# Attention kernel with a recorded schedule: the third bank of a ScalarE group lent to VectorE, another unit order, and scheduler constants by stage

## Chip, cores, metric

One core of one Trainium2 chip. The metric is the device time of one execution in microseconds.

## The reference, cut to what matters

Four attention layers run in turn over 2048 tokens of width 512, with 32 heads of 16: A, B, A, B with the same weights twice. A attends within segments of 512 tokens under a causal mask and adds a linear memory of earlier segments. B attends over all 2048 tokens.

```python
x = x + _A_ref(_layernorm(x), A_wq, A_wk, A_wv, A_wo, A_beta)
x = x + _B_ref(_layernorm(x), B_wqkv, B_wo)
x = x + _A_ref(_layernorm(x), A_wq, A_wk, A_wv, A_wo, A_beta)
x = x + _B_ref(_layernorm(x), B_wqkv, B_wo)
# in B: scores = q @ k^T * Dh**-0.5 ; p = softmax(scores) ; o = p @ v     (A: the same in segments, masked, plus memory)
```

The exponentials of the scores are most of the work: 32 heads of 2048 x 2048 for each B layer.

## The kernel before

The program is recorded by a scheduler in Python. It keeps a clock for each engine, advances them by constants, and at each step picks what TensorE issues next: a group of score tiles, a PV batch (the matmuls of four finished tiles with V), or a step of a background thread (projections, layer norm, memory). The order that it records is then fixed: each engine executes its own list in order, held by semaphores. A wrong constant makes no wrong result, only an order that suits the chip badly.

PSUM has eight banks: two halves of three for score groups, two for projections and for accumulating PV. TensorE fills one half while ScalarE reads the other.

```python
DX_AHEAD = 0.696; DX_SLACK = 4.004; MMC = 0.22; PV0 = 0.33; PB = 0.027; DVE_AHEAD = 4.525; RATE = 0.762; CF = 0.684   # (cut; one line each)
PAT = ["AAAAAAAA", "ABABABABBBABAAABBA", "AAAABBBBAAAA", "AAABABABABAA", "AAABABABABAA", "BBABAABAAA"]   # order of units in each block

def form(self):                                   # the next group for ScalarE (cut)
    n = 3 if m == "w" or self.half == 0 else 2    # "w": threes; else threes and twos in turn

def emit_group(self, tiles, mode):                # (cut)
    # a score matmul for each tile, each into a bank of its own and on its own 32 rows of the array
    self.dx_scores(tiles, mode)                   # perhaps one more tile, for VectorE
    # ONE activation over all the banks of the group
    o = sc.add("act", lambda e: e.activation(dst, src, ACT.Exp, scale=float(SCALE)), ...)

def dx_scores(self, tiles, mode):                 # (cut)
    bank = self.free_bank()
    t = sc.t["pe"]
    if bank.t_free + 0.3 > t or sc.t["dve"] > t + self.dx_ahead(...) or not self.dx_room():
        return
    self.dx_score([x["pv"][0][2] for x in tiles], bank, SC1)    # one matmul, one VectorE eviction
```

After four such evictions VectorE computes the batch's exponential in seven operations over 2048 columns (`g_dx`), and the batch's PV joins the queue.

The softmax here doesn't subtract the row's maximum and nothing guards it: scores larger than these inputs give would overflow.

Of the kernel before, what the change touches and what calls it, by code (L numbers as in the profile page):

```python
# [25 lines left out]
EXP_C = SCALE * 1.4426950408889634  # L26
EXP_A, EXP_B, EXP_D = 10.0720224, 43.9353157, 125.459638
DX_AHEAD = 0.696
DX_SLACK = 4.004
DX_LEAD = 69  # L30
MMC = 0.22
SC0, SC1 = 0.33, 0.02
PV0 = 0.33
PB = 0.027
DVE_AHEAD = 4.525
MAXPV = 3
RATE = 0.762
LAST = 3
HAM_W = 3.4133
HAM_T = 5.0  # L40
# [4 lines left out]
CF = 0.684  # L45
# [1 line left out]
T_ISS = 1.3  # L47
D_LAT = 2.5
QMASK = True
PAT = ["AAAAAAAA", "ABABABABBBABAAABBA", "AAAABBBBAAAA", "AAABABABABAA", "AAABABABABAA", "BBABAABAAA"]  # L50
M3 = "m"
LN_G = 3
DX_WIDE = True


class Op:
# [227 lines left out]
class KernelBuilder:  # L284
# [810 lines left out]
            tl["nblk"] = {"0": 4, "13": 4, "22": 4}[tl["masks"]]  # L1095
        return u

    def emit_group(self, tiles, mode):
        sc = self.sc
        self.mode = mode  # L1100
        lo = self.bank_lo
        banks = [self.banks[lo + i] for i in range(len(tiles))]
        alloc = self.new_alloc()
        n = len(tiles)
        s0 = self.slot_for(n)
        self.slot = s0 + n
        for k in range(max(len(tl["sc"]) for tl in tiles)):
            for i, tl in enumerate(tiles):
                if k >= len(tl["sc"]):
                    continue  # L1110
                lhsT, rhs, off, N, reads = tl["sc"][k]
                out = self.ps[:, banks[i].col0 + off:banks[i].col0 + off + N]
                sc.add("pe", (lambda out, lhsT, rhs: lambda e: e.matmul(out, lhsT, rhs, start=True, stop=True))(out, lhsT, rhs),  # L1113
                       reads=reads, bank_ops=[(banks[i], "w", alloc)], emit=False, name="S", cost=((SC0 if k == 0 else N / 2400.0) if i == 0 else SC1),
                       cold=N / 2400.0 if i == 0 else 0.0, work=0.14 * N / 512)
        self.dx_scores(tiles, mode)
        W = 512 * n
        src = self.ps[:, banks[0].col0:banks[0].col0 + W]
        dst = self.pT[:, s0:s0 + n, :].rearrange("p a b -> p (a b)")
        o = sc.add("act", lambda e: e.activation(dst, src, ACT.Exp, scale=float(SCALE)), writes=[self.b_pT[s0 + i] for i in range(n)],  # L1120
                   bank_ops=[(b, "r", alloc) for b in banks], name="E", cost=0.065 + W / 1200.0)
        for b in banks:
            b.t_free = o.t_end
        t_rdy = o.t_end
        i = 0
        while i < n:
            m = tiles[i]["masks"]
            k = i + 1
            while m == "0" and k < n and tiles[k]["masks"] == m:
                k += 1  # L1130
            if m is not None:
                if m == "0":
                    ap = self.pT[:, s0 + i:s0 + k, 0:128]
                    pat = [[0, k - i], [1, 128]] if k - i > 1 else [[1, 128]]
                    if k - i == 1:
                        ap = self.pT[:, s0 + i, 0:128]
                    cnt = k - i
                else:
                    base = self.pT[:, s0 + i:s0 + i + 1, 0:1]
                    ap = bcast_ap(base, [[384 if m == "13" else 256, 2], [1, 128]])  # L1140
                    pat = [[0, 2], [1, 128]]
                    cnt = 2
                om = sc.add("pool", (lambda ap, pat: lambda e: e.affine_select(ap, ap, pattern=pat, compare_op=ALU.is_ge, fill=0.0, base=0,  # L1143
                                                                            channel_multiplier=-1))(ap, pat),
                            reads=[self.b_pT[s0 + x] for x in range(i, k)], writes=[self.b_pT[s0 + x] for x in range(i, k)],
                            name="K", cost=0.2 + 0.115 * cnt)
                t_rdy = om.t_end
            i = k
        for i, tl in enumerate(tiles):
            tl["slot"] = s0 + i  # L1150
        for tl in tiles:
            self.slot_use[tl["slot"]] = tl.get("nblk", 1)
            self.pvt.append(tl)
            uu = tl["u"]
            if len(self.pvt) == 4:
                uu["pq"].append(dict(tiles=self.pvt, t=t_rdy, dx=False))
                self.pvt = []
            self.tile_scored(uu)
# [38 lines left out]
    def dx_ahead(self, u, need):  # L1197
# [4 lines left out]
        for tl, _ in self.upq:  # L1202
            if tl["u"]["kind"] == "B" and tl["u"]["no"] > u["no"]:
                break
            n += 1
        return DVE_AHEAD if 0.45 * n < need + DX_SLACK else DX_AHEAD

    def dx_scores(self, tiles, mode):

        sc = self.sc  # L1210
        if ("op", 0, 3) not in self.ev or len(tiles) < 2:
            return
        if self.dx_tiles is None:
            four = self.dx_pick()
            if four is None:
                return
            self.dx_tiles = four
            self.dx_left = [2, 3, 0, 1]
        bank = self.free_bank()
        t = sc.t["pe"]  # L1220
        if bank.t_free + 0.3 > t or sc.t["dve"] > t + self.dx_ahead(self.dx_tiles[0]["u"], 7.5 + 1.4 * len(self.dx_left)) or not self.dx_room():
            return
        self.dx_score([x["pv"][0][2] for x in tiles], bank, SC1)

# [108 lines left out]
    def pv_group(self):  # L1333
# [14 lines left out]
        if u["qm"]:  # L1348
            sc.t["pe"] += 0.1
            for tl in g["tiles"]:  # L1350
                for b in tl["pv"]:
# [3 lines left out]
                    if not g["dx"]:  # L1355
# [3 lines left out]
                                                                                stop=True, skip_group_check=True))(o0, w, v, first),  # L1359
                           reads=[br] + vreads, bank_ops=[(bank, "w", alloc)], emit=False, name="W", cost=PB)  # L1360
                    first = False
            if g["dx"]:
                op.emit = True
        else:
            n = len(g["tiles"][0]["pv"])
            for k, i in ((k, i) for k in range(n) for i in range(4)):
# [5 lines left out]
                else:  # L1372
# [4 lines left out]
                       reads=[br] + vreads, bank_ops=[(bank, "w", alloc)], emit=g["dx"] and i == 3, name="V",  # L1377
                       cost=0.0 if i else PV0 if k == 0 else N / 2400.0, cold=0.0 if i else N / 2400.0, work=0.16 * N / 512)
        if g["dx"]:
# [197 lines left out]
    def units(self):  # L1577
# [3 lines left out]

        seq = [(A(0, 0, "m") + A(0, 1, "m"), [], PAT[0])]
        seq += [(A(0, 2, "m") + A(0, 3, "m"), F(1, 0, 4, "a", "m") + F(1, 4, 8, "m", "m"), PAT[1])]
        seq += [(F(1, 8, 12, "m", "m") + F(1, 12, 16, "b", "w") + B(1, 0, "w", NPART), [], "")]
        for qc in range(1, 4):
            b = B(1, qc, "w")
            seq += [(b, A(2, qc - 1, "w"), PAT[1 + qc])]
        a3 = F(3, 0, 12, "a", M3)
# [5 lines left out]
    def build(self):  # L1594
        self.alloc()
        self.cnt = {}
        self.late = []
        self.slot = 0
        self.slot_use = [0] * RING
        self.pvt = []  # L1600
        self.ln_owner = None
        self.setup()
        self.out_batches = [self.new_batch(f"out{s}") for s in range(4)]
        for L in range(LAST + 1):
            self.spawn_layer(L)
        sc = self.sc
        self.log = []
        self.blocks = [[list(a), list(b), list(pat)] for a, b, pat in self.units()]
        self.blocks = [[[x for x in q if x[0]["L"] <= LAST] for q in b[:2]] + [b[2]] for b in self.blocks]
        for i, (u, _) in enumerate(x for b in self.blocks for x in b[0] + b[1] if x[0]["kind"] == "B"):  # L1610
            u["no"] = i
        self.upq = []
        self.half = 0
        self.mode = "n"
        self.act_ok = True
        self.run()
        self.act_ok = True
        self.acc_bank = None
        self.mode = "n"
        while self.threads:  # L1620
            self.ensure_any()
        for s in range(4):
            bt = self.out_batches[s]
            sc.add("sp", (lambda bt: lambda e: e.wait_ge(bt.sem, bt.total))(bt), name="fin")
        sc.finalize()
# [103 lines left out]
    def run(self):  # L1729
        sc = self.sc  # L1730
        credit = 0.0
        g = None
        while True:
# [4 lines left out]
            t = sc.t["pe"]  # L1738
# [38 lines left out]
            if rs is not None and rs <= t + eps and not (credit >= 1.0 and bg is not None):  # L1777
                tiles, m = g
                self.bank_lo = 3 * self.half
                self.half ^= 1  # L1780
                del self.upq[:len(tiles)]
                L = tiles[0]["u"]["L"]
                self.act_ok = m == "m" and L < 2
                self.emit_group(tiles, m)
                credit = min(credit + (RATE if self.act_ok else 0.0), 2.0)
                self.log.append((len(self.log), L, tiles[0]["u"]["s"], m, round(sc.t["act"], 2), round(sc.t["pe"], 2), round(sc.t["dve"], 2),
                                 round(sc.t["pool"], 2), self.backlog(), len(tiles)))
                g = None
                continue
            if rp is not None and rp <= t + eps and self.backlog() >= MAXPV:  # L1790
# [27 lines left out]
            if KEEP and self.acc_open and t + d <= tc + KEEP_D and (0.0 if sc.warm else KEEP0) <= sc.lately() < KEEP and self.pvu and self.pvu[0]["L"] <= KEEP_L:  # L1818
                self.keep_warm()
                continue  # L1820
            sc.t["pe"] = to

    def keep_warm(self):

# [75 lines left out]
```

## Time and profile before

| | before |
|---|---|
| median of the runs beside the changed kernel | 2096.53 us (2092.73 to 2097.51, 4 runs) |
| span of the profiled run | 2094.3 us |
| busy: ScalarE, TensorE, VectorE | 95%, 83%, 77% |
| score tiles on ScalarE, on VectorE | 4316, 420 |
| ScalarE groups of three, of two | 1312, 188 |

Read it as one bound engine with a feeder: ScalarE's time is its number of tiles and groups times their fixed costs, plus whatever it waits for scores. The lines are in the prediction.

### The profile page before, as it was taken

How to read it: one execution, taken by the hardware profiler on the slowest of the kernel's cores; microseconds unless marked ns; L12 is line 12 of the kernel's file. 1: busy time of each engine (PE TensorE's matmuls, PEld its weight loads, DVE VectorE, ACT ScalarE, POOL GpSimd, SP SyncE). 2: the span in 40 equal slices, each digit the busy share in tenths (PEclk: the TensorE clock that was granted, in tenths of full speed). 3: DMA queues.
4: the chain of work that ended last, by engine and by line, in shares of the span. 5: the costliest groups of instructions: out<-in, count | busy, mean ns of one | idle time of the engine just before them, and what ended most of it. 6: DMA issues, size and time to landing. Idle time of an engine off the chain costs nothing.

```text
span 2094.3 us, 41469 instructions
## 1 busy us (share of the span) xinstructions
PE 1732.3 (83%) x17382; PEld 589.3 (28%) x17382; DVE 1605.0 (77%) x2447; ACT 1997.3 (95%) x1595; POOL 248.1 (12%) x563
## 2 busy tenths in 40 slices
PE   7779988888877888878888888888888888888887
PEld 2222221111221122121222223223444433443443
DVE  6887668886647777777768578688788988897984
ACT  5879989999999999999999999999999999999998
POOL 4542320000130002110021103200000000000000
PEclk9779876567565575576765788575655565555555
DMA  4210100001000000010000100100000000000000
GB/s 121 51 32 11 31 11 1 1 1 21 1 11 11 11 11 1 1 16 18 8 1 1 21 11 1 22 1 2 14 5 4 4 14 4 5 4 14 7 5 11
DMA packets 75467, 27.31 MB, mean 13 GB/s; under 512 B 68112, under 2 KB 74768, under 8 KB 75280
## 3 DMA queue, kind: packets, MB, share of 16 engines
q1 hardware_dynamic: 74176, 23.62, 5.2%
q8 instruction: 136, 2.23, 0.4%
q10 hardware_dynamic: 1104, 1.05, 0.2%
q14 instruction: 51, 0.42, 0.1%
HBM read 6.30 MB, written 2.10 MB: 4 GB/s over the span
## 4 chain that ended last, share of the span: by engine, by line
ACT 48%; PE 30%; issue 10%; DVE 9%; POOL 1%; DMA 1%; SPq 0%; ACTq 0%; DVEq 0%; POOLq 0%
ACT pT L1120 47%; PE ps L1113 12%; PE ps L610 8%; PE ps L1358 5%; PE ps L1376 4%; PE ps L1246 2%; POOL pT L1143 1%; DMA xT<-xn 1%; DVE T L1496 1%; DVE lnst L647 1%; DVE dz L1249 1%; DVE ot L904 0%; DVE ph L771 0%; SPq L429 0%; DVE df L1286 0%
## 5 line engine op out<-in xcount | busy, mean ns | idle before, releaser
L1120 ACT ACTIVATE pT<-ps 128x1536 bf16<-128x1536 f32 (+1 forms) x1504 | 1962.6, 1487 | 69.0 <-PE ps L1113 59.3
L1113 PE MATMUL ps<-q,kB 32*128 32x512 bf16 x3676 | 696.0, 548 | 262.3 <-ACT pT L1120 254.5
L1249 DVE TENSOR_SCALAR dz<-ps 128x512 int32<-128x512 f32 x420 | 289.8, 690 | 153.5 <-PE ps L1246 139.5
L1113 PEld LDWEIGHTS ps<-q,kB 32*128 32x128 bf16 x3676 | 129.9, 97 | 698.5 <-ACT pT L1120 648.7
L1376 PE MATMUL ps<-pT,vB 128*17 128x512 bf16 x2228 | 286.0, 515 | 2.3 <-DVE ot L904 1.3
L1143 POOL TENSOR_SCALAR_AFFINE_SELECT pT<-pT 128x256 bf16<-128x256 bf16 (+2 forms) x515 | 219.5, 455 | 549.2 <-ACT pT L1120 547.9
L1246 PE MATMUL ps<-q,kB 32*128 32x512 bf16 x420 | 243.3, 579 | 0.0
L1358 PEld LDWEIGHTS ps<-vB,pT 128*128 128x128 bf16 x5792 | 181.2, 104 | 169.9 <-issue 169.3
L1358 PE MATMUL ps<-vB,pT 128*128 128x17 bf16 x5792 | 214.2, 176 | 0.0
L1113 PE MATMUL ps<-q,kA 32*128 32x512 bf16 (+3 forms) x1024 | 125.0, 391 | 40.4 <-ACT pT L1120 38.6
L1286 DVE TENSOR_SCALAR df<-dz 128x2048 f16<-128x2048 uint16 x105 | 129.3, 1232 | 3.0
L1376 PEld LDWEIGHTS ps<-pT,vB 128*17 128x17 bf16 x2228 | 52.1, 90 | 204.7 <-issue 191.4
L1293 DVE TENSOR_SCALAR db<-dz 128x2048 int16<-128x2048 int16 x77 | 94.0, 1221 | 2.8 <-PE ps L1376 2.8
L1496 DVE STREAM_TRANSPOSE T<-ps 128x512 f32<-128x512 f32 x94 | 66.6, 709 | 24.7 <-PE ps L1376 24.2
L610 PE MATMUL ps<-xT,wB 128*128 128x512 bf16 x256 | 80.1, 445 | 0.8 <-DVE dz L1249 0.8
L610 PE MATMUL ps<-xT,wA 128*128 128x512 bf16 x256 | 73.6, 417 | 6.0 <-DVE T L1496 2.0
L976 DVE TENSOR_TENSOR x_tok<-x_tok,ps 128x512 bf16<-128x512 bf16 x60 | 41.1, 686 | 42.4 <-PE ps L610 42.3
L655 POOL TENSOR_SCALAR lnr<-lnmv 128x4 f32<-128x4 f32 x15 | 5.2, 344 | 550.1 <-DVE lnmv L650 550.1
L1298 DVE TENSOR_TENSOR tokk<-tokk,df 128x2048 f16<-128x2048 f16 x57 | 69.5, 1219 | 0.7
L1302 DVE TENSOR_TENSOR tokk<-tokk,df 128x2048 f16<-128x2048 f16 x57 | 69.4, 1218 | 0.6
L1113 PEld LDWEIGHTS ps<-q,kA 32*128 32x128 bf16 x1024 | 29.6, 99 | 118.9 <-ACT pT L1120 92.2
L625 DVE CAST q<-ps 128x512 bf16<-128x512 f32 x53 | 36.4, 686 | 34.5 <-PE ps L610 34.4
(128 smaller groups left out, 1541.2 us busy)
## 6 DMA issues: line engine op xcount, KB each, us to landing
x_tok<-in_A_x_dram SPq DMA_DIRECT2D x14, 128.0 KB, 2.7
wB<-in_B_wqkv_dram SPq DMA_DIRECT2D x4, 384.0 KB, 4.1
out_dram<-x_tok SPq DMA_DIRECT2D x3, 512.0 KB, 2.9
xT<-xn SPq DMA_TRANSPOSE x60, 2.4
wA<-in_A_wk_dram SPq DMA_DIRECT2D x1, 512.0 KB, 7.7
wA<-in_A_wq_dram ACTq DMA_DIRECT2D x1, 512.0 KB, 8.1
wA<-in_A_wv_dram SPq DMA_DIRECT2D x1, 512.0 KB, 9.0
woA<-in_A_wo_dram SPq DMA_DIRECT2D x1, 512.0 KB, 8.0
```

Source lines behind the costliest of these rows:

```text
L610: return self.sc.add("pe", lambda e: e.matmul(out, lhsT, rhs, start=start, stop=stop), reads=reads, bank_ops=[(bank, "w", alloc)], emit=la ...
L1113: sc.add("pe", (lambda out, lhsT, rhs: lambda e: e.matmul(out, lhsT, rhs, start=True, stop=True))(out, lhsT, rhs), reads=reads, bank_ops=[ ...
L1120: o = sc.add("act", lambda e: e.activation(dst, src, ACT.Exp, scale=float(SCALE)), writes=[self.b_pT[s0 + i] for i in range(n)], bank_ops= ...
L1143: om = sc.add("pool", (lambda ap, pat: lambda e: e.affine_select(ap, ap, pattern=pat, compare_op=ALU.is_ge, fill=0.0, base=0, channel_mult ...
L1246: sc.add("pe", lambda e: e.matmul(out, lhsT, rhs, start=True, stop=True), reads=reads, bank_ops=[(bank, "w", alloc)], emit=True, name="SX" ...
L1249: o = sc.add("dve", lambda e: e.tensor_scalar(dst, out, float(EXP_C * 65536.0), -126.0 * 65536.0, op0=ALU.mult, op1=ALU.max), writes=[self ...
L1286: o = dv(lambda e: e.tensor_scalar(F, lo, 2.0 ** -16, -0.5, op0=ALU.mult, op1=ALU.add), bz, bF, "dF", 1.24)
L1293: o = dv(lambda e: e.tensor_scalar(E, hi, 128.0, 16256.0 + 53.0, op0=ALU.mult, op1=ALU.add), bz, bE, "dE", 1.24)
L1298: o = dv(lambda e: e.tensor_tensor(Pz, Pz, F, ALU.mult), bF + bP, bP, "dP2", 1.24)
L1358: op = sc.add("pe", (lambda o0, w, v, first: lambda e: e.matmul(self.ps[:, o0:o0 + 17], w, v, start=first, stop=True, skip_group_check=Tru ...
L1376: sc.add("pe", (lambda out, v, rhs, start, stop: lambda e: e.matmul(out, v, rhs, start=start, stop=stop, skip_group_check=True))(out, v, r ...
L1496: o = sc.add("dve", lambda e: e.transpose(T1.rearrange("p b r -> p (b r)"), src), writes=[bT], bank_ops=[(bank, "r", alloc)], name="T1", c ...
```

## The change

The intent: let VectorE take a tile when the only free bank is the one that the group itself would use, and set the scheduler's constants by stage (by number of ScalarE groups issued), with a new order of units in three of the blocks.

```diff
-PAT = ["AAAAAAAA", "ABABABABBBABAAABBA", "AAAABBBBAAAA", "AAABABABABAA", "AAABABABABAA", "BBABAABAAA"]
+PAT = ["AAAAAAAA", "ABABABABBBABAAABBA", "BAAABBBAAAAA", "AAAAABABABAB", "AAAABABABBAA", "BBABAABAAA"]
+DX3 = 1
+TUNE = [
+    (0, {'CF': 0.829, 'PB': 0.02, 'DX_AHEAD': 0.5, 'DX_SLACK': 4.776, ..., 'RATE': 0.606, 'MMC': 0.22, 'PV0': 0.371, 'DX3': 1}),
+    (110, {'CF': 0.849, 'RATE': 0.472, 'MMC': 0.229}),
+    ...                                                  # nine more stages
+    (1430, {'PB': 0.035, 'DX_LEAD': 53, 'DVE_AHEAD': 3.961, 'MAXPV': 2}),
+]
...
+    def dx_scores(self, tiles, mode, spare=None):
+        if len(tiles) < 2 or not self.dx_wanted():       # dx_wanted: the tests on VectorE, as before
+            return
+        bank = spare or self.free_bank()
+        if spare is None and bank.t_free + 0.3 > sc.t["pe"]:
             return
...
                 self.bank_lo = 3 * self.half
+                spare = None
+                if DX3 and len(tiles) == 3 and (DX3 == 2 or self.free_bank().t_free + 0.3 > t) and self.dx_wanted():
+                    ...
+                    tiles, spare = tiles[:2], self.banks[self.bank_lo + 2]
...
-                self.emit_group(tiles, m)
+                self.emit_group(tiles, m, spare)
```

CF is the scheduler's surcharge for a matmul at the slow clock; PB, PV0 and MMC are costs of PV and projection matmuls; the others are thresholds and, for RATE, how often a background step goes before a score group.

More of the change, by code (lines that the diff above doesn't have):

```diff
@@ L28 @@
 DX_AHEAD = 0.696
-DX_SLACK = 4.004
+DX_SLACK = 4.776
 DX_LEAD = 69
@@ L32 @@
 SC0, SC1 = 0.33, 0.02
-PV0 = 0.33
-PB = 0.027
+PV0 = 0.371
+PB = 0.026
 DVE_AHEAD = 4.525
 MAXPV = 3
-RATE = 0.762
+RATE = 0.606
 LAST = 3
@@ L53 @@
 DX_WIDE = True
+DX3 = 1
+TUNE = [
+    (0, {'CF': 0.829, 'PB': 0.02, 'DX_AHEAD': 0.5, 'DX_SLACK': 4.776, 'DX_LEAD': 69, 'DVE_AHEAD': 4.525, 'MAXPV': 3, 'RATE': 0.606, 'MMC': 0.22, 'LN_G': 3, 'PV0': 0.371, 'DX3': 1}),
+    (110, {'CF': 0.849, 'RATE': 0.472, 'MMC': 0.229}),
+    (220, {'MMC': 0.213, 'PV0': 0.365}),
+    (330, {'LN_G': 2}),
+    (440, {'DVE_AHEAD': 2.5}),
+    (660, {'PB': 0.022}),
+    (880, {'PB': 0.026, 'RATE': 0.4}),
+    (990, {'MMC': 0.2, 'PV0': 0.324}),
+    (1100, {'CF': 1, 'PB': 0.025, 'DX_AHEAD': 0.676, 'LN_G': 3}),
+    (1210, {'PB': 0.036, 'DX_LEAD': 64, 'DVE_AHEAD': 3.61}),
+    (1320, {'DX_SLACK': 5.687}),
+    (1430, {'PB': 0.035, 'DX_LEAD': 53, 'DVE_AHEAD': 3.961, 'MAXPV': 2}),
+]
 class Op:
@@ L1096, in unit_A, with emit_group @@
         return u
-    def emit_group(self, tiles, mode):
+    def emit_group(self, tiles, mode, spare=None):
         sc = self.sc
@@ L1115, in emit_group @@
                        cold=N / 2400.0 if i == 0 else 0.0, work=0.14 * N / 512)
-        self.dx_scores(tiles, mode)
+        self.dx_scores(tiles, mode, spare)
         W = 512 * n
@@ L1206, in dx_ahead, with dx_wanted @@
         return DVE_AHEAD if 0.45 * n < need + DX_SLACK else DX_AHEAD
-    def dx_scores(self, tiles, mode):
+    def dx_wanted(self):
         sc = self.sc
-        if ("op", 0, 3) not in self.ev or len(tiles) < 2:
-            return
+        if ("op", 0, 3) not in self.ev:
+            return False
         if self.dx_tiles is None:
@@ L1215, in dx_scores @@
             if four is None:
-                return
+                return False
             self.dx_tiles = four
             self.dx_left = [2, 3, 0, 1]
-        bank = self.free_bank()
-        t = sc.t["pe"]
-        if bank.t_free + 0.3 > t or sc.t["dve"] > t + self.dx_ahead(self.dx_tiles[0]["u"], 7.5 + 1.4 * len(self.dx_left)) or not self.dx_room():
+        return sc.t["dve"] <= sc.t["pe"] + self.dx_ahead(self.dx_tiles[0]["u"], 7.5 + 1.4 * len(self.dx_left)) and self.dx_room()
+    def dx_scores(self, tiles, mode, spare=None):
+        sc = self.sc
+        if len(tiles) < 2 or not self.dx_wanted():
+            return
+        bank = spare or self.free_bank()
+        if spare is None and bank.t_free + 0.3 > sc.t["pe"]:
             return
@@ L1615, in build @@
         self.act_ok = True
+        self.tune = list(TUNE)
+        self.retune()
         self.run()
@@ L1779, in run @@
                 self.bank_lo = 3 * self.half
+                spare = None
+                if DX3 and len(tiles) == 3 and (DX3 == 2 or self.free_bank().t_free + 0.3 > t) and self.dx_wanted():
+                    if any(x is tiles[2] for x in self.dx_tiles) or self.upq[2][0] is not tiles[2]:
+                        raise RuntimeError("a tile of the group was taken")
+                    tiles, spare = tiles[:2], self.banks[self.bank_lo + 2]
                 self.half ^= 1
@@ L1787, in run @@
                                  round(sc.t["pool"], 2), self.backlog(), len(tiles)))
+                self.retune()
                 g = None
@@ L1821, in run, with retune @@
             sc.t["pe"] = to
+    def retune(self):
+        while self.tune and self.tune[0][0] <= len(self.log):
+            globals().update(self.tune.pop(0)[1])
     def keep_warm(self):
```

## The prediction

> **What bounds the kernel now.** I read the page first: engine shares, then the 40 slices.
>
> ```profile
> span 2094.3 us, 41469 instructions
> PE 1732.3 (83%) x17382; PEld 589.3 (28%) x17382; DVE 1605.0 (77%) x2447; ACT 1997.3 (95%) x1595; POOL 248.1 (12%) x563
> ...
> ACT  5879989999999999999999999999999999999998
> ...
> PEclk9779876567565575576765788575655565555555
> ```
>
> ScalarE (ACT) is busy 95% of the span and in nearly every slice after the first four. TensorE (PE) is second, and for half of the program at a granted clock near half speed. So the end is set by ScalarE's own work plus the 97 us (2094.3 - 1997.3) in which it idles. The groups say what that work is:
>
> ```profile
> L1120 ACT ACTIVATE pT<-ps 128x1536 bf16<-128x1536 f32 x1312 | 1800.4, 1551 | 52.7 <-PE ps L1113 46.3 <-POOL pT L1143 1.7 <-PE ps L1246 1.7
> ...
> L1249 DVE TENSOR_SCALAR dz<-ps 128x512 int32<-128x512 f32 x420 | 289.8, 690 | 153.5 <-PE ps L1246 139.5 <-PE ps L1358 3.8 <-PE ps L1376 1.4
> ...
> L1120 ACT ACTIVATE pT<-ps 128x1024 bf16<-128x1024 f32 x188 | 198.3, 1056 | 9.5 <-PE ps L1113 6.1 <-POOL pT L1143 2.9
> ```
>
> The softmax exponential of a score tile (512 columns, one PSUM bank) goes to ScalarE in groups of three tiles (1312) or two (188), or to VectorE (DVE), four tiles to a batch: 420 evictions, 105 batches. A tile moved to VectorE is taken off the bound engine.
>
> Recorded durations overlap, so the cost is read from start to start, in ScalarE's timeline:
>
> ```profile
> 94.55 1.45 ACT L1120 ACTIVATE pT<-ps 128x1536 bf16<-128x1536 f32 x1
> 95.88 0.61 ACT L623 ACTIVATE q<-ps 128x512 bf16<-128x512 f32 x1
> 97.13 0.63 ACT L765 ACTIVATE et<-tokk 128x512 bf16<-128x512 bf16 x1 [0.65 <-DVE tokk L771]
> 97.66 1.01 ACT L1120 ACTIVATE pT<-ps 128x1024 bf16<-128x1024 f32 x1
> 98.57 0.62 ACT L765 ACTIVATE ph<-q 128x512 bf16<-128x512 bf16 x1
> ...
> 1968.19 115.97 ACT L1120 ACTIVATE pT<-ps 128x1536 bf16<-128x1536 f32 x86 [0.18 <-PE ps L1113]
> ```
>
> A group of three holds the engine 1.33 us (95.88 - 94.55), a group of two 0.91 (98.57 - 97.66). In the long run at the end it is (115.97 - 1.45)/85 = 1.347 a group, so there ScalarE is at its floor. I use 1.345 and 0.92: a tile costs 0.425 and a group about 0.07 by itself.
>
> Last, the waits of ScalarE:
>
> ```profile
> ACT pT L1120 <- PE ps L1113: 59.3, 59, 6.8
> ACT xT L707 <- PE ps L699: 7.5, 2, 7.3
> ACT pT L1120 <- POOL pT L1143: 4.7, 6, 2.1
> ```
>
> The listed idle is nearly all "no scores yet". Split by 100 us, ScalarE idles 27.8, 14.9 and 6.6 in the first three, under 7 in each later one, and 9.7 in the last, of which the tail after its last exponential is most. About 20 us at the front (first scores at 19.5 us) and 10 at the end are out of this change's reach. The scores come late because of what TensorE does in between; its own timeline:
>
> ```profile
> 906.55 1.03 PE L1113 MATMUL ps<-q,kB 32*128 32x512 bf16 x6
> 907.52 0.60 PE L1358 MATMUL ps<-vA,pT 128*128 128x17 bf16 x16
> 907.97 1.77 PE L610 MATMUL ps<-xT,wB 128*128 128x512 bf16 x4
> ```
>
> A score group occupies about 0.54 us at the slow clock, a PV batch about 0.5, a projection of four matmuls 1.8. A projection beside a PV batch, between two score groups, outlasts one ScalarE group (1.345) and part of the one buffered ahead.
>
> **What the Trainium skill says.** "ScalarE: Activation LUTs", What ACT_TABLE_LOAD costs: an ACTIVATE with immediate operands takes 186 ns + 0.833 ns per column, and neighbours overlap by about 93. That gives 1373 and 946 ns; the trace's 1345 and 910 are near, and the difference per tile agrees (427 against about 425). "TensorEngine Tiling (Array Packing)", PSUM Bottleneck: use ScalarE and VectorE both for the eviction once tiling has sped up TensorE; that is what the kernel does, and the trace agrees that eviction is the bound. "PSUM — Partial Sum Buffer", Specifications: the two may read PSUM in parallel if they don't collide on a bank, so VectorE may hold the third bank while ScalarE reads the first two; no run yet shows this. "TensorE: Matmul & The Clock Gate", Part 1: the clock is half speed after an idle window, so faster feeding does not follow from fewer matmuls; the clock row's fives agree.
>
> **The change part by part.** The scheduler records a fixed program, so I counted instructions in both programs.
>
> (1) The third bank. Before, a VectorE tile needed a free bank of the miscellaneous set (in the phase of three-tile groups, the one of two that is not accumulating PV). Now, if that is busy and VectorE has room, a three-tile group gives ScalarE two tiles, and its third bank goes to VectorE. This happens 78 times, 60 of them in the second, third and fourth query chunks of the first attention-B layer and the A units woven into them. Groups go from 1312 threes and 188 twos to 1254 and 267; ScalarE tiles from 4316 to 4300. Sum: -58 x 1.345 + 79 x 0.92 = -78.0 + 72.7 = **-5.3 us of ScalarE**, all on the path. Sixteen tiles at 0.425 would be 6.8, but 21 more groups take 1.5 back. Copies on ScalarE go from 37 to 36, about -0.5.
>
> (2) VectorE gets four batches. Each is 4 x 0.690 for eviction and seven operations of 1.232, 1.221, 0.687, 1.219, 0.693, 1.220 and 1.220 = 7.49 by their rows, together 10.25 us; **+41 us**, 1605 to 1646, 79% of the span. It lies beside ScalarE. In the last attention layer VectorE is already busy 85 to 88%, and only one of the four net batches lands there.
>
> (3) TensorE. Matmuls stay at 17384; the 21 extra score groups take 21 x 0.54 = 11 us, beside ScalarE.
>
> (4) The constants and unit patterns move projections. I counted gaps between successive score groups holding a projection of four or more matmuls and also a PV batch, or eight or more projection matmuls: **165 before, 126 after**. Most of the drop is in the first 220 groups (68 to 46); in the rest 97 become 80. Total score waits without the first 6.8 are 52.5 us, so 52.5/165 = 0.32 us for each heavy gap (an estimate that charges all waits to them). 39 fewer make **-12 us**.
>
> (5) A cost. Behind a two-tile group the next scores are due 0.43 us sooner. Where the kernel alternates threes and twos today, 32 groups starting at 1362.5 us took 38.26 us: (38.26 - 1.02)/31 = 1.20 a group, against a floor of (1.345 + 0.92)/2 = 1.13. That is 0.07 us lost per group, twice this per two-tile group at worst; 79 more cost 79 x 0.07 = **+5.5 us**.
>
> Sum: -5.3 - 0.5 - 12 + 5.5 = -12.3, that is 2084. I lower this to 2082, since constants set separately for twelve stages look fitted to this kernel, and such fitting tends to find more than a count of gaps does.
>
> **The rivals.** *The two-tile groups starve ScalarE.* TensorE is busy 83%, so per 1.345 us it needs about 1.1; behind a two-tile group it has 0.92, and the third bank comes back only after VectorE's eviction. For: the PEclk fives, in just the stages where most of the 78 lie. Against: two groups are buffered, and short groups are one in nine there. If each costs 0.3 us more, 78 x 0.3 = 23: 2105.
>
> *VectorE becomes the bound.* If the later batches come late, PV and the layer's end wait. For: 85 to 88% in the last layer. Against: 77% overall, and the row of the eviction shows 153.5 us of idle waiting for scores. With 41 us more work and a quarter exposed: 2092.
>
> *The schedule gain is much larger.* If half of the roughly 60 us of idle between front and tail went, with part (1): 2096.5 - 30 - 6 = 2060. For: the constants of the scheduler's clock model rise (0.684 to 0.829 and later 1.0), nearer to the slow clock that the trace shows. Against: the idle is spread, under 2% in most stretches after 300 us.
>
> **Range and chances.** Faster by over 2% means under 2054.6, a gain of 42 us: all of part (1) plus 36 of the 60 us of reachable idle; I give 5%. Slower by over 2% needs every rival cost at once, 2%. The range 2064 to 2097 runs from nearly the large gain to nothing gained.
>
> **What would show it.** The exponential's groups at 1254 and 267 with unchanged durations, and ScalarE busy about 6 us down. ScalarE's wait on scores from 59 to near 47, most of the drop in the first 300 us. VectorE busy near 1646. The middle stages (300 to 1200 us) should gain from moved tiles and lose a little in waits behind two-tile groups; the last layer (1400 on) should gain only some 2 us. I am wrong if waits grow where the short groups are, if the granted clock shifts enough to change matmul durations, or if the gain sits in the last layer.

## The result and the profile after

The changed kernel took 2081.40 us (2080.47 to 2084.30, 4 runs) against 2096.53: ratio 0.9934, 95% interval 0.9916 to 0.9951. Repeated later on another occasion it took 2083.65 against 2093.39: 0.9951 (0.9939 to 0.9964). So the gain is 0.5 to 0.7%, clear of noise and within 2%. The kernel before ran slow on the first occasion: its medians beside the later experiments are 2092.06, 2093.67 and 2093.39. The gain in medians was 15.1 us then and 9.7 us in the repeat. The granted clock is not the cause of the whole: at a mean clock of 0.649 the kernel before took 2090.5 to 2093.2 us (8 runs), the changed one 2081.1 to 2084.3 (5 runs). Ratios here are the mean time of one kernel's fast runs over that of the other's of the same rounds, so not quite the ratio of the medians quoted.

The page of the changed kernel, engine shares and slices:

```profile
span 2082.3 us, 41423 instructions
PE 1705.9 (82%) x17296; PEld 592.2 (28%) x17382; DVE 1645.9 (79%) x2492; ACT 1990.4 (96%) x1615; POOL 253.3 (12%) x564
...
ACT  6879899999999999999999999999999999999997
...
PEclk9679897557565675557776797675655555555555
```

The span is 12.0 us shorter; ScalarE is busy 6.9 us less and idle 91.9 instead of 97.0. VectorE is busy 40.9 us more. TensorE's busy time can't be compared: 86 matmul records are missing from this trace (17296 of 17382).

Its groups, with shapes kept apart (count | busy us, mean ns | idle before, releasers):

```profile
L1135 ACT ACTIVATE pT<-ps 128x1536 bf16<-128x1536 f32 x1254 | 1731.7, 1540 | 44.4 <-PE ps L1128 38.1 <-PE ps L1267 2.3 <-POOL pT L1158 1.3
L1270 DVE TENSOR_SCALAR dz<-ps 128x512 int32<-128x512 f32 x436 | 301.0, 691 | 156.8 <-PE ps L1267 143.6 <-PE ps L1128 2.9 <-PE ps L1379 1.2
L1135 ACT ACTIVATE pT<-ps 128x1024 bf16<-128x1024 f32 x267 | 287.5, 1083 | 15.1 <-PE ps L1128 12.7 <-POOL pT L1158 1.8 <-PE ps L1267 0.4
```

Counts are those of the program, and the eviction takes what it took (691 ns). The idle time before threes fell (52.7 us to 44.4, the part behind scores 46.3 to 38.1) and rose before twos (9.5 to 15.1, behind scores 6.1 to 12.7), where the new short groups are. ScalarE's waits (us in total, times, longest):

```profile
ACT pT L1135 <- PE ps L1128: 57.4, 62, 6.6
ACT xT L722 <- PE ps L714: 7.6, 2, 7.4
ACT et L780 <- DVE sm L914: 4.0, 1, 4.0
```

The first was 59.3: nearly the same. And the third bank in use, in the timeline of all engines:

```profile
610.37 0.60 PE L1128 MATMUL ps<-q,kB 32*128 32x512 bf16 x2
610.37 0.60 PE L1267 MATMUL ps<-q,kB 32*128 32x512 bf16 x1
610.91 0.61 PE L1397 MATMUL ps<-pT,vB 128*17 128x512 bf16 x4
611.08 0.69 DVE L1270 TENSOR_SCALAR dz<-ps 128x512 int32<-128x512 f32 x1 [0.81 <-PE ps L1267]
```

and ScalarE's own timeline, where this group is the first of six that the view puts in one line:

```profile
611.10 7.94 ACT L1135 ACTIVATE pT<-ps 128x1024 bf16<-128x1024 f32 x6
```

Two matmuls for ScalarE and one for VectorE start in the same instant here, so the third tile costs TensorE no time of its own. ScalarE reads the first two banks (from 611.10) while VectorE reads the third (from 611.08), and results are correct. Neither takes longer: over the 78 such groups the median eviction is 0.692 us (0.693 for the others), and the shortest activation that overlaps an eviction is 1.017 us, like the shortest that does not. The prediction had this from the Trainium skill, "PSUM — Partial Sum Buffer", Specifications, and could not yet show it.

**Where the time went, by stage.** Listed idle hides delays shorter than the overlap of two records, so I took every ScalarE instruction from the trace, start to start, and subtracted a floor: 1.345 us for a group of three, 0.918 for two, 0.49 for one, 0.48 for a copy, 0.52 for the exponentials of the A memory. What is left I call loss. (The floors are near, not exact: the median start to start of a three is 1.330 us in both traces. So loss is understated somewhat, alike in both.) "Front" is the first 220 groups, "last" is from the second query chunk of the last layer on, where no attention-A units are left, and "middle" is between, where A units and projections are woven into B.

| | total floor | total loss | front: time, loss | middle: time, loss | last: time, loss |
|---|---|---|---|---|---|
| before | 1983.8 | 91.9 | 328.4, 48.6 | 1138.1, 31.3 | 609.2, 12.0 |
| changed | 1977.9 | 84.8 | 322.0, 43.1 | 1133.6, 29.3 | 607.1, 12.4 |

The 13.0 us between these are 5.9 of floor and 7.1 of loss, and 5.5 of the loss is in the front. These are single executions; how far two of them differ in one stage is shown under the prediction's heavy gaps below. (The span fell by 12.0; the rest lies before the first and after the last ScalarE instruction.)

### The profile page after: what moved, and what is told of

Its sections match the earlier page's. It is cut to its first block, busy times and chain, and to the rows that moved or that the text cites. A ratio compares the mean times of both kernels' runs of the same rounds, so it can differ in the third digit from the quotient of the medians.

```text
span 2082.3 us, 41423 instructions
## 1 busy us (share of the span) xinstructions
PE 1705.9 (82%) x17296; PEld 592.2 (28%) x17382; DVE 1645.9 (79%) x2492; ACT 1990.4 (96%) x1615; POOL 253.3 (12%) x564
## 4 chain that ended last, share of the span: by engine, by line
ACT 49%; PE 29%; issue 11%; DVE 7%; POOL 2%; DMA 1%; SPq 0%; ACTq 0%; DVEq 0%; POOLq 0%
ACT pT L1135 48%; PE ps L1128 13%; PE ps L625 6%; PE ps L1379 5%; PE ps L1397 4%; POOL pT L1158 2%; PE ps L1267 1%; DMA xT<-xn 1%; DVE lnst L662 1%; DVE T L1517 0%; DVE tokk L786 0%; ACT ph L780 0%; DVE ot L919 0%; SPq L444 0%; DVE db L1325 0%
## 5 line engine op out<-in xcount | busy, mean ns | idle before, releaser
L1135 ACT ACTIVATE pT<-ps 128x1536 bf16<-128x1536 f32 (+2 forms) x1525 | 1957.3, 1458 | 66.1 <-PE ps L1128 57.4
L1128 PE MATMUL ps<-q,kB 32*128 32x512 bf16 x3660 | 699.6, 546 | 256.3 <-ACT pT L1135 248.3
L1270 DVE TENSOR_SCALAR dz<-ps 128x512 int32<-128x512 f32 x436 | 301.0, 691 | 156.8 <-PE ps L1267 143.6
L1158 POOL TENSOR_SCALAR_AFFINE_SELECT pT<-pT 128x256 bf16<-128x256 bf16 (+2 forms) x516 | 223.8, 463 | 613.4 <-ACT pT L1135 611.9
L1397 PE MATMUL ps<-pT,vB 128*17 128x512 bf16 x2216 | 278.7, 507 | 0.7 <-DVE q L640 0.5
L1267 PE MATMUL ps<-q,kB 32*128 32x512 bf16 x436 | 250.0, 573 | 0.0
L1307 DVE TENSOR_SCALAR df<-dz 128x2048 f16<-128x2048 uint16 x109 | 134.0, 1229 | 2.4
L625 PE MATMUL ps<-xT,wB 128*128 128x512 bf16 x228 | 70.4, 429 | 7.4 <-issue 3.9
L625 PE MATMUL ps<-xT,wA 128*128 128x512 bf16 x238 | 68.7, 412 | 8.1 <-issue 2.1
L991 DVE TENSOR_TENSOR x_tok<-x_tok,ps 128x512 bf16<-128x512 bf16 x60 | 41.0, 686 | 41.6 <-PE ps L625 41.3
L680 DVE TENSOR_SCALAR xn<-x_tok,lnmv,lnr 128x512 bf16<-128x512 bf16 x60 | 24.5, 429 | 50.3 <-DMA xT<-xn 49.4
L1325 DVE TENSOR_TENSOR db<-db,dz 128x2048 int16<-128x2048 int16 x51 | 62.8, 1231 | 1.2
```

Of the source, the lines that this page charges most:

```text
L625: return self.sc.add("pe", lambda e: e.matmul(out, lhsT, rhs, start=start, stop=stop), reads=reads, bank_ops=[(bank, "w", alloc)], emit=la ...
L1128: sc.add("pe", (lambda out, lhsT, rhs: lambda e: e.matmul(out, lhsT, rhs, start=True, stop=True))(out, lhsT, rhs), reads=reads, bank_ops=[ ...
L1158: om = sc.add("pool", (lambda ap, pat: lambda e: e.affine_select(ap, ap, pattern=pat, compare_op=ALU.is_ge, fill=0.0, base=0, channel_mult ...
L1267: sc.add("pe", lambda e: e.matmul(out, lhsT, rhs, start=True, stop=True), reads=reads, bank_ops=[(bank, "w", alloc)], emit=True, name="SX" ...
L1270: o = sc.add("dve", lambda e: e.tensor_scalar(dst, out, float(EXP_C * 65536.0), -126.0 * 65536.0, op0=ALU.mult, op1=ALU.max), writes=[self ...
L1307: o = dv(lambda e: e.tensor_scalar(F, lo, 2.0 ** -16, -0.5, op0=ALU.mult, op1=ALU.add), bz, bF, "dF", 1.24)
```

## The experiments

Each kernel ran 5 rounds against the kernel before; all results were correct. "Deep gap" below means 12 or more projection matmuls (those of the A memory counted with them) between two successive score groups, counted in the program's order.

**1. third_alone** (constants and patterns of before):

```diff
-PAT = [... "BAAABBBAAAAA", "AAAAABABABAB", "AAAABABABBAA", ...]      # and the new constants
+PAT = [... "AAAABBBBAAAA", "AAABABABABAA", "AAABABABABAA", ...]      # and the old ones, TUNE = []
```

> The third bank with the constants and unit patterns of before. Counted: 1257 threes and 265 twos (ScalarE floor 1935.4 us against 1939.2 before), 72 third-bank groups, heavy gaps 153 against 165. Theory C (the constants carry the gain; the third bank's saving of floor is eaten by what ScalarE loses behind the short groups, 78 x 0.11 us in the changed kernel's trace): 2095, within 4 of before. Rival T (the third bank carries the gain): 2086 or lower.

Measured: 2145.26 us against 2092.06, ratio 1.0250 (1.0237 to 1.0263). Both theories fall: it is 53 us slower than having none of the change.

**2. consts_alone** (the constants, old patterns, no third bank: `DX3 = 0`):

> The constants by stage, with no third bank and the old patterns. Counted: floor 1944.7 us (12 more tiles on ScalarE than before), heavy gaps 130. Theory C: the heavy gaps pay 35 x 0.24 = 8 and the floor costs 5.5, so 2093 or lower. Rival T: 2097 to 2102, since the floor is higher and the constants were fitted to a schedule with the third bank.

Measured: 2125.87, ratio 1.0159 (1.0146 to 1.0172). Both fall again.

**3. no_third** (the changed kernel with `DX3 = 0`, in the constant and in the stages):

> The changed kernel with the third bank switched off, constants and patterns kept. Counted: floor 1939.2 us as before, 4316 tiles, heavy gaps 143 as counted the same way (127 with the third bank). Theory C: 2082 to 2086, for the floor rises 5.5 and the loss behind short groups (10) goes. Rival T: 2092 or more.

Measured: 2105.63, ratio 1.0059 (1.0045 to 1.0074). The number suits theory T, but T is refuted by run 1.

**4. third_always** (the changed kernel with `DX3 = 2`):

> The changed kernel, taking the third bank whenever VectorE wants a tile, even when another bank is free: 225 such groups instead of 78, 1154 threes and 418 twos, floor 1936.8 (3.1 above the changed kernel), tiles 4300 alike, heavy gaps 109. If a third-bank group costs ScalarE 0.11 us beyond its floor (theory C), 147 more cost 16, less 4 for heavy gaps: 2096. Rival T (the short group is nearly free): 2081 to 2084.

Measured: 2131.75, ratio 1.0186 (1.0172 to 1.0200). Neither.

Hardly any of the extra loss is in the front or the last stage. By the same reckoning:

| | front loss | middle loss | last loss |
|---|---|---|---|
| third_alone | 44.2 | 90.1 | 11.6 |
| consts_alone | 41.4 | 63.9 | 10.5 |
| no_third | 43.8 | 48.6 | 8.0 |
| third_always | 41.0 | 71.5 | 16.2 |

In the middle, ScalarE stands still a few times for long. Its waits in third_alone:

```profile
ACT pT L1122 <- PE ps L1115: 101.3, 71, 12.3
ACT pT L1122 <- PE ps L1254: 15.1, 8, 11.1
```

The longest, 12.3 us, ends at 1272.40 us. TensorE's timeline before it:

```profile
1257.85 0.39 PE L1115 MATMUL ps<-q,kB 32*128 32x512 bf16 x2 [0.20 <-ACT pT L1122]
1258.17 0.40 PE L1384 MATMUL ps<-pT,vB 128*17 128x512 bf16 x4
1258.50 1.90 PE L612 MATMUL ps<-woB,oT 128*128 128x512 bf16 x8
1260.32 1.04 PE L612 MATMUL ps<-xT,wB 128*128 128x512 bf16 x4
1261.19 0.61 PE L612 MATMUL ps<-wB,xT 128*128 128x128 bf16 x8
1261.73 0.61 PE L1384 MATMUL ps<-pT,vB 128*17 128x512 bf16 x8
1265.41 0.62 PE L612 MATMUL ps<-wB,xT 128*128 128x128 bf16 x8 [3.07 <-DVE kB L627]
1265.87 1.45 PE L612 MATMUL ps<-xT,wB 128*128 128x512 bf16 x4
1271.76 0.61 PE L1115 MATMUL ps<-q,kB 32*128 32x512 bf16 x3 [4.44 <-DVE kB L627]
```

Between two score groups (L1115) stand 32 projection matmuls, and twice TensorE waits for VectorE to evict keys, the second time for keys that the score group itself needs. The recorded order had come to a unit whose keys were not yet made, so a whole string of dependent work had to pass first. Such deep gaps can be counted without running: one in before, two in the changed kernel, five in third_alone. ScalarE's loss just in front of third_alone's four new ones is 7.2, 10.7, 11.3 and 12.6 us, together 42 of the 53. consts_alone has five deep gaps too; their losses, 2.4 to 6.3 us, come to 23.5. That gave theory D: the order of units makes or avoids deep gaps, and a schedule's worth is decided there.

no_third has no new deep gap, though. Its longest stop in the middle, in the timeline of all engines:

```profile
985.88 1.89 PE L625 MATMUL ps<-xT,wA 128*128 128x512 bf16 x4
...
990.98 1.22 DVE L1325 TENSOR_TENSOR db<-db,dz 128x2048 int16<-128x2048 int16 x1
...
992.26 0.61 PE L1397 MATMUL ps<-db,vB 128*17 128x512 bf16 x4 [4.50 <-DVE db L1325]
992.86 0.60 PE L1397 MATMUL ps<-pT,vB 128*17 128x512 bf16 x4
...
994.17 2.82 ACT L1135 ACTIVATE pT<-ps 128x1536 bf16<-128x1536 f32 x2 [6.20 <-PE ps L1128]
```

TensorE reached the PV of a VectorE batch and waited there 4.5 us, until the batch's last operation had ended. The score group recorded behind it had to wait too, and ScalarE with it, for 6.2 us. Counting matmuls does not show this one.

**5. third_pat** (third_alone with the new patterns in place of the old):

> The third bank and the new unit patterns, with the constants of before: third_alone with its patterns exchanged. Counted: floor 1933.6 us, 77 third-bank groups, heavy gaps 143, and one deep gap (12 or more projection matmuls between two score groups) as in before, where third_alone has five. Theory D (third_alone lost its 50 us in four new deep gaps that the pattern's order of units makes or avoids): 2091, within 5 of before: floor -5.6, heavy gaps -5, short groups +9. Rival X (the third bank itself, or the old constants with it, cost the 50 us): 2125 to 2145.

Measured: 2110.35 against 2093.67, ratio 1.0070 (1.0058 to 1.0083). Of third_alone's extra 53 us, 17 are left: the exchange of patterns alone took 36 away. But D's number is missed by 19 us.

**6. pat_alone** (the kernel before with the new patterns):

> The kernel before with only the new unit patterns. Counted: floor, heavy gaps (165) and deep gaps (1) all as before. Theory D: 2092, within 4 of before. Rival: the new patterns are worth 10 us by themselves, 2082.

Measured: 2106.14, ratio 1.0050 (1.0036 to 1.0064). Missed by 14, with every count the same. Its waits of TensorE on VectorE's batches, in the middle (330 to 1490 us; total us, times, longest), and below it those of before (330 to 1470 us):

```profile
PE ps L1376 <- DVE db L1304: 6.2, 6, 4.6
```

```profile
PE ps L1376 <- DVE db L1304: 1.9, 6, 0.5
```

One of the six is 4.6 us long, and at the same place ScalarE stands for 6.4 us: the late batch again, in an order whose counts look harmless.

**7. old_pat** (the changed kernel with the old patterns):

> The changed kernel with the old unit patterns. Counted: floor 1939.1 (5.4 above the changed kernel), 73 third-bank groups, heavy gaps 125, one new deep gap (20 projection matmuls before a group of the last attention layer). Theory D: 2081 + 5.4 + about 8 for the deep gap = 2095. Rival C (constants and third bank carry the gain whatever the pattern): 2081 to 2086.

Measured: 2109.73, ratio 1.0069 (1.0055 to 1.0083). The changed kernel without its patterns is slower than before. The loss at its new deep gap is 1.8 us in the trace, not the 8 expected: the count of matmuls alone does not set the cost of a gap.

**8. one_stage** (the changed kernel with only the first entry of `TUNE`):

> The changed kernel with its first set of constants kept throughout, no change by stage. Counted: floor 1942.8 (9.1 above), 86 third-bank groups, two new deep gaps of 28 and 36 projection matmuls near groups 891 and 918. Theory D: 2081 + 9 + 20 = 2110. Rival C2 (the constants by stage matter little): 2081 to 2088.

Measured: 2130.42, ratio 1.0170 (1.0156 to 1.0184). The middle loss is 65.5 us.

D puts one_stage last of these four, rightly, but third_pat first, wrongly, and is 14 to 20 us too low for each. What all of 1 to 8 have in common is a middle loss of 43 to 90 us where before and the changed kernel have about 30. Each of the two looks fitted as a whole, and a part of one set into the other lands on an order with some stops of 3 to 13 us. If so, a comparison of parts taken singly measures mostly the misfit, not the part; run 9 tests this for the third bank.

That also showed in the scheduler's own clock, which is a number of the recording and not of the chip. With the old constants it ended at 2076, 2121, 2084 and 2077 for before, third_alone, pat_alone and third_pat: 16 to 34 us short of the measured times. With the new ones it ended at 2083, 2105, 2136, 2128 and 2104 for the changed kernel, no_third, third_always, consts_alone and old_pat: within 6 us of each (one_stage, with the first set of them, ends at 2124 and is 6 short). With the changed constants the scheduler foresees most of the stops that it makes. The old ones were not blind: as a difference from before they foresaw 45 of third_alone's 53 us, but 8 of pat_alone's 12 and 1 of third_pat's 17. So the first surprise could have been read off the recording, and was not. So a fair test of the third bank was possible: fit the kernel without it as well.

**9. no_third_fit** (`DX3 = 0`; cost constants kept; patterns and thresholds searched by the scheduler's clock):

```diff
-PAT = ["AAAAAAAA", "ABABABABBBABAAABBA", "BAAABBBAAAAA", "AAAAABABABAB", "AAAABABABBAA", "BBABAABAAA"]
+PAT = ["AAAAAAAA", "ABBABABABBBAAABAAB", "BAAABBBAAAAA", "AAAAAABAABBB", "AAAABBBABAAA", "ABBBABAAAA"]
-    (110, {'CF': 0.849, 'RATE': 0.472, 'MMC': 0.229}),            # and other thresholds by stage
+    (110, {'CF': 0.849, 'RATE': 0.472, 'MMC': 0.229, 'DVE_AHEAD': 2.416, 'DX_SLACK': 5.28}),
```

> No third bank, the changed kernel's constants for costs kept, its unit patterns and its other constants searched anew (some 11,500 schedules tried in four searches, judged by the scheduler's own clock, which ended 2104 for no_third against 2105.6 measured). Counted: floor 1939.1, heavy gaps 142, two deep gaps; the scheduler's clock ends at 2088.4. If the third bank is worth only what it takes off the floor and out of the waits once both schedules are fitted: 2088, 7 above the changed kernel. Rival N (the third bank is worth nothing, a fit alone gives the gain): 2081. Rival G (the scheduler's clock can be fitted without the chip following): 2100 or more.

Measured: 2090.03 (2089.40 to 2092.28) against 2093.39, ratio 0.9983 (0.9970 to 0.9995). The chip followed the clock (2088.4). Run 3 differs from this one in patterns and thresholds alone, and took 2105.63: some 16 us of what it seemed to show for the bank was misfit.

**10. third_fit** (third bank kept, searched the same way from the changed kernel):

```diff
-PAT = [... "AAAABABABBAA", "BBABAABAAA"]
+PAT = [... "AAAABBABABAA", "BBABAABAAA"]                            # and other thresholds by stage
```

> With the third bank, searched the same way from the changed kernel (some 15,300 schedules). Counted: floor 1932.1 (1.6 under the changed kernel), 83 third-bank groups, one deep gap; the scheduler's clock ends at 2078.1 against 2082.9 for the changed kernel. If the chip follows the clock: 2077, 5 under the changed kernel. Rival G: 2085 to 2100.

Measured: 2082.03 (2079.22 to 2083.93), ratio 0.9942 (0.9928 to 0.9955). That lies between the two forecasts: of the 4.8 us that the clock promised, 1.6 came, as much as its floor is lower. The two intervals overlap, so it does not clearly beat the changed kernel.

**11. after_again** (the changed kernel, as a yardstick):

> The changed kernel once more, in the rounds of the two above, as their yardstick: 2081, within 2.

Measured: 2083.65 (2082.82 to 2085.44), ratio 0.9951 (0.9939 to 0.9964).

Runs 9 and 11 together: with both schedules fitted, the third bank is worth 2090.0 - 2083.7 = **6.4 us** (8.0 against third_fit), and searched patterns and constants without it 2093.4 - 2090.0 = **3.4 us**. The stages say where:

| | total floor | front loss | middle loss | last loss |
|---|---|---|---|---|
| no_third_fit | 1981.4 | 43.6 | 33.0 | 9.3 |
| after_again | 1977.9 | 42.3 | 31.5 | 10.3 |
| third_fit | 1976.2 | 41.1 | 33.5 | 9.2 |

3.5 of the 6.4 us are floor, the rest about 2 of loss, which single traces hardly resolve, and small remainders outside the ScalarE sequence. A longer search could improve either schedule, so 6.4 is the worth between these two fits and no bound.

## Why the prediction was right

The time was 2081.4 for a predicted 2082.0. Step by step:

**The bound and its floor: right.** ScalarE remained the bound. The change of floor was predicted at -5.3 - 0.5 and is 5.9 by the stages, with ScalarE busy 6.9 less. 78 third-bank groups brought only 16 tiles to VectorE, since the ordinary route to a free bank was used less. third_always shows more: with 225 such groups VectorE gets the same 436 tiles. So there it is no longer free banks that limit the number; that the tests on VectorE's own time and buffers do is likely, and was not tested alone.

**VectorE: right.** Predicted 1646 us busy, measured 1645.9. It did not become the bound. The last stage took 2.1 us less, as predicted (some 2).

**TensorE: not shown.** The predicted extra 11 us can't be read, since 86 records are missing. (The prediction's 17384 matmuls are 17382 in both programs.)

**Heavy gaps: right in sum, wrong in its parts.** Predicted: 39 fewer at 0.32 us, so -12. The loss from the group before a heavy gap to the next ScalarE instruction went from 39.6 us at 165 gaps to 27.8 at 126: -11.8. A heavy gap costs 0.24 and 0.22 us and not 0.32, as not every wait was theirs; but the average hides deep gaps, of which the changed kernel has one more than before (16 matmuls, 3.9 us). "ScalarE's wait on scores from 59 to near 47" failed: it is 57.4. New waits behind short groups took the place, and part of the gain is delay that no listed wait shows.

Where it falls is wrong by this count: 22 of the 39 gaps are in the front, but the loss fell by 2.3 us there and by 9.5 after it (6.1 and 9.2 with the copies inside the gaps). The whole loss did fall most in the front, 5.5 of 7.1, of which 3.3 at copies; but these are single executions. The third bank is first used at group 248 and the patterns differ only later, so before, pat_alone, third_alone and third_pat have the same program for the first 220 groups (as rebuilt from the recorded kernels). They lost 48.6, 48.4, 44.2 and 46.0 us there. The changed kernel, its repeat, consts_alone, no_third, old_pat and third_fit share another one: 43.1, 42.3, 41.4, 43.8, 41.3 and 41.1. So two executions of one order differ by up to 4.4 us, and the front's gain, about 4.6 on average, is the constants' alone. The granted clock is a rival here, and one that the prediction named: in the first 350 us it was 0.81 to 0.83 in the first four kernels and 0.85 to 0.87 in the others. Whether fewer gaps or faster matmuls gave the front's gain stays open.

**Short groups: right kind, predicted too small.** Predicted 0.07 us each, +5.5. The loss behind the 78 third-bank groups is 8.9 us (0.113 each; 0.144 in the repeat), and 1.4 more behind the groups after them: about +10. This is gross: a group of three loses 0.034 on average in before, so what a short group adds is nearer 0.08. In the last stage of third_always, where no projection interferes, it is 0.076 for each of 100. The rival of starving ScalarE was thus partly true, well short of its 0.3 us each. The prediction's reading of the clock row for it is off: 12 of the 78 lie in the last layer, where the fives stand together; most of the others lie in the middle, where the clock is 0.65 on average (350 to 1480 us). Nor do the fives show the idle windows that the prediction takes from the Trainium skill, "TensorE: Matmul & The Clock Gate", Part 1: from 1500 to 2000 us in before the clock is 0.53 with TensorE busy 84% and no wait longer than 1.0 us.

**The lowering from 2084 to 2082: luck.** The terms sum to -7.4 with the measured sizes (-5.9 - 11.8 + 10.3) where floor and loss fell by 13.0; the other 5.6 us are smaller losses at groups of neither kind and at ScalarE's copies in the front (21.3 us before, 18.0 after). The base was luck as well: the forecast gain of 14.5 us met 15.1 on the first occasion and 9.7 in the repeat.

**What the prediction had no thought of:** that the parts are not additive. It summed them as if each could be had alone; alone the third bank costs 53 us, the constants 34, the patterns 12. Its hint was there, in the rival of the larger gain: the constants of the scheduler's clock move toward the measured clock. The runs show that this agreement, within 6 us where it was 16 to 34 off, goes with the changed constants; that it is what made the better fit findable is likely and not shown, since how the constants were found is not part of this case.

## What to carry to other kernels

In a kernel whose order is recorded by a scheduler, test a part of a change only after fitting the rest to it again; otherwise the test may measure the misfit, which here was over twice the effect of the bank (16 us against 6). Count, before running, the work that stands between two feeds of the bound engine, and look first for the few deepest gaps and for instructions ordered ahead of a result that comes late: on an engine that takes its list in order, one of these stops everything behind it. Look at the scheduler's own clock before running a part: here it foresaw most of the worst surprise. Make the scheduler's clock agree with the chip on kernels that it was not fitted to, and only then search with it.

## What the Trainium skill lacked or had wrong

- "ScalarE: Activation LUTs", What ACT_TABLE_LOAD costs: its figures give 1373 and 946 ns from start to start for 1536 and 1024 columns; the runs show a median of 1330 (mean 1347 in a long run) and 903 to 920. In the pair shown neighbours overlap by 0.12 us (a record of 1.45 us with the next start after 1.33), not 0.093.
- "TensorEngine Tiling (Array Packing)", PSUM Bottleneck: advises both engines for the eviction, but not what dividing a group costs the larger one: about 0.07 us for the extra instruction, and 0.08 (last stage of third_always) to 0.14 (repeat of the changed kernel) of waiting behind the shorter group.
- No page that I read gives the cost of what decided most here: one late operand in TensorE's order holds the score groups recorded behind it (a 4.5 us wait for a VectorE batch became 6.2 us on ScalarE), and deep gaps of 12 or more projection matmuls cost 7 to 13 us each in third_alone.
- No page that I read covers a TensorE that is busy at half clock: 0.53 granted from 1500 to 2000 us in before, busy 84% by the records, longest wait 1.0 us.
